# Block 0: transposes of the output weights and the gate product one slice further back in TensorE's queue

## Chip, cores and metric

The kernel runs on one core of a Trainium2 chip. The metric is the device time of one execution in microseconds (us). TensorE is named PE in the rows, its weight load PEld, VectorE DVE, ScalarE ACT, GpSimd POOL, and the queue that issues transfers SP.

## What is computed

A linear-attention recurrence (4 batches, 8 heads of 48, 768 steps), a gated feed-forward layer on the 3072 resulting rows, and a routed layer with 8 experts that picks one expert for each row:

```
for t in range(S):
    cur = np.einsum('bhd,bhe->bhde', u[None] * kt, vt)
    y[:, :, t] = np.einsum('bhd,bhde->bhe', rt, state + cur)
    state = w[None, :, :, None] * state + np.einsum('bhd,bhe->bhde', kt, vt)
...
g = x @ w_gate
silu = g * (1.0 / (1.0 + np.exp(-g)))
val = x @ w_val
return (silu * val @ w_out).astype(np.float32)
...
logits = x @ w_gate
e_idx = np.argmax(logits, axis=1)
...
    h = np.maximum(x[mask] @ w1[e], 0.0)
    ye = h @ w2[e]
    out[mask] = gate_w[mask, None] * eom[mask, e, None] * ye
```

## The kernel before

The 3072 rows are 24 tiles of 128; three tiles are a block, and there are 8 blocks. The feed-forward layer goes through 12 slices f of 128 hidden columns. Each slice of a block has gate products on TensorE into bank 3 (L494, nine matmuls), value products into bank 4 (L494, nine more), a silu on ScalarE (L502), its product with the value on VectorE (L503), a cast to the high part h on ScalarE (L505), a subtraction for the low part (L506, on GpSimd in block 0), and two slices later the down products into banks 0 to 2 (L513).

Block 0 also prepares the weights, once. They come as 64-bit words. Slice f is converted on VectorE by nine instructions (L214, L215, L216: `conv_a`) into a buffer `cv` of which there are two, one for even and one for odd slices. ScalarE casts the result to the high part of W (L232, the weight cast), GpSimd subtracts for the low part (L233: `conv_b`). So that the router's logits come out of the down products too, the output weights are multiplied with the router matrix G: three transposes on TensorE into bank 7 (L241) and a copy of them to `gt` on ScalarE (L243: `gate_a`); then three matmuls with G, also into bank 7 (L249, the gate product of the weights), small copies on ScalarE (L252, L253) and a small subtraction on GpSimd (L254: `gate_b`).

Between these steps lies the attention of the next block's three tiles (i = 3, 4, 5 in block 0): scaling of k and r on VectorE (L316), a diagonal (L334, then L343 on GpSimd or eight L341 on ScalarE), scores on TensorE into banks 6 and 7 in turn (L363), a masking of the diagonal's tile with them on VectorE (L368), output matmuls into bank 6 (L376, L390), a state product into bank 7 (L427), the evacuation of the output (L410 on ScalarE, L411 on VectorE), and the state update out of bank 7 (L441, L443).

Each engine carries out its instructions in the order in which the program writes them. That order is set by hand: a block has 24 slots, two to a slice. Slot 2f is written after the gate products of slice f, ahead of the down products of f-2 and the value products of f; slot 2f+1 after the silu, product and casts of slice f. `a_place` appends the attention's steps to the slots, and the lines below `if blk == 0` put the weights' steps in, mostly at the front of a slot. Semaphores make an instruction wait for its data and for the bank or buffer that it overwrites.

Of the kernel before, what the change touches and what calls it, by code (L numbers as in the profile page):

```python
# [28 lines left out]
NF = DFF // P  # L29
# [22 lines left out]
def kernel(  # L52
# [167 lines left out]
    def conv_a(f):  # L220
        for u in conv_steps(f):
            u()
# [3 lines left out]
    def conv_b(f, parts=(ALL,)):  # L226
        x = cvs[f]
        if f not in W:
            W[f] = wpool.tile([P, 2, FG], F32R, tag=f"W{f}", name=f"W{f}")
        for o in parts:  # L230
            hi, lo = W[f][:, 0, o], W[f][:, 1, o]
            act.copy(out=hi, in_=x[:, o])  # L232
            pool.tensor_tensor(out=lo, in0=x[:, o], in1=hi.bitcast(F32), op=ALU.subtract)  # L233
# [11 lines left out]
    def gate_b(f):  # L245
        t = gts.pop(f)
        wg = bank[7][:, DM : DM + 16]
        for c in range(KC):
            pe.matmul(wg, t[:, c * P : (c + 1) * P], G[:, c, :], start=(c == 0), stop=(c == KC - 1))  # L249
        hi, lo = W[f][:, 0, FW:], W[f][:, 1, FW:]  # L250
        x = apool.tile([P, 16], F32, tag="wg", name="wg", bufs=2)
        act.copy(out=x, in_=wg)  # L252
        act.copy(out=hi, in_=x)  # L253
        pool.tensor_tensor(out=lo, in0=x, in1=hi.bitcast(F32), op=ALU.subtract)  # L254
# [177 lines left out]
    def a_state_up(i, b):  # L432
        c = i // NB
        if c == TPB - 1:
            return
        m4 = bank[b][:, 0 : 4 * HD].rearrange("s (p e) -> s p e", p=4)
        for j in range(2):
            q = slice(64 * j, 64 * j + HD)
            sv, m = Sst[i % NB][q, :, j, 0:HD], m4[q]
            if c == 0:  # L440
                dve.tensor_copy(out=sv, in_=m)  # L441
            else:
                dve.tensor_tensor(out=sv, in0=m, in1=sv, op=ALU.add)  # L443
# [169 lines left out]
    def a_place(slots, i, first):  # L613
        e = 1 if i % BT == BT - 1 else 0
        if i + 1 < NT:
            slots[first].append(lambda: a_load(i + 1))
        if i < 2 * BT:
            slots[first + (i == BT)].append(lambda: a_scale(i))
            slots[first + 1].append(lambda: a_diag(i, BT < i))
            slots[first + 3 - e] += [lambda: a_keys(i), lambda: a_scores(i), lambda: a_mask(i)]  # L620
            slots[first + 5 - e] += [lambda: a_out(i), lambda: a_load_kr(i + 1), lambda: a_bonus(i + 1)]
            slots[first + 6].append(lambda: a_state_up(i, 7))
            return
        e = 0
        if i == 2 * BT:
            slots[first] += [lambda: a_scale(i), lambda: a_diag(i, False)]
            slots[first + 2] += [lambda: a_scores(i), lambda: a_next(i), lambda: a_load_kr(i + 1)]
        slots[first + 3 - e].append(lambda: a_keys(i))
        if i + 1 < NT:
            slots[first + 3 - e].append(lambda: a_bonus(i + 1))  # L630
            slots[first + 4 - e].append(lambda: a_scale(i + 1))
        slots[first + 5 - e].append(lambda: a_burst(i))
        if i + 1 < NT:
            slots[first + 5 - e].append(lambda: a_diag(i + 1, False))
            slots[first + 6 - e].append(lambda: a_next(i + 1))
        if i + 2 < NT:
            slots[first + 6 - e].append(lambda: a_load_kr(i + 2))
# [165 lines left out]
    with tc.manual_schedule():  # L803
# [56 lines left out]
        zts = []  # L860
        for blk in range(NBLK):
# [6 lines left out]
                for t in range(BT):  # L868
                    a_place(slots, (blk + 1) * BT + t, 8 * t)
            if blk == 0:  # L870
                slots[0][0:0] = [lambda: gate_b(0), lambda: conv_b(1, (GV, OUT)), lambda: gate_a(1), lambda: conv_a(2), lambda: a_state(0, 0)]
                slots[1][0:0] = [lambda: gate_b(1), lambda: conv_b(2), lambda: a_state(1, 1)]
                slots[2][0:0] = [lambda: gate_a(2), lambda: a_state(2, 2), lambda: gate_b(2)]
                for f in range(3, NF):
                    slots[2 * f - 5] += [lambda f=f: conv_a(f), lambda f=f: next_w(f + 2) if f > 3 else None]
                    slots[2 * f - 3].insert(0, lambda f=f: conv_b(f)); slots[2 * f - 3 + (f == 3)].insert(0, lambda f=f: gate_a(f))
                    slots[2 * f - 2].insert(0, lambda f=f: gate_b(f)) if f > 3 else slots[4].append(lambda: gate_b(3))
                slots[19].append(lambda: zts.append(late_consts()))
            else:
                for o, u in zip((4, 7, 7) if blk == NBLK - 1 else (12, 15, 15), c_units(blk - 1)):  # L880
                    slots[o].append(u)
                if blk == 1:
                    for i in range(16):
                        clear(2 * i, 2 + (2 * i) // 3)
                if 2 <= blk < 6:
                    for n in range(3):
                        for k, u in enumerate(scan_units(3 * (blk - 2) + n)):
                            slots[7 * n + 1 + 4 * k].append(u)
# [279 lines left out]
```

## Time and profile before

| what | before |
|---|---|
| median of 3 runs | 862.46 us (859.89 to 864.29) |
| the profiled execution, its own time | 861.56 us |
| its span, first to last instruction | 859.8 us |
| TensorE, matmuls busy | 821.9 us, 96% of the span |
| VectorE busy | 459.8 us, 53% |
| ScalarE busy | 271.2 us, 32% |
| GpSimd busy | 267.9 us, 31% |
| mean granted clock of TensorE | 0.985 |

Busy shares are means over the whole span, in which block 0 takes the time from about 34 to 135 us. The granted clock is a share of full speed: 1.00 is 2.4 GHz and 0.50 is 1.2 GHz.

### The profile page before, as it was taken

Reading aid. Unit: us, or ns where it says so; the run is one execution under the profiler, and the core shown is the slowest. Engines: PE = TensorE matmul, PEld = TensorE weight load, DVE = VectorE, ACT = ScalarE, POOL = GpSimd, SP = SyncE. Lnnn points to the kernel's source line nnn. Section 1 sums busy time; section 2 is a strip of 40 time slices with the busy share of each in tenths; the row PEclk is TensorE's granted clock in tenths of the full one; section 3 lists DMA queues with packets and bytes.
Section 4 is the critical chain, followed back from the end, with each engine's and each line's share of the span. In section 5 each row is a group of like instructions: output and inputs, shape, how many; then the busy total and the mean of one; then the engine's idle time right before and its main releaser. Section 6 shows DMA issues by size and latency. Waiting matters only on the chain.

```text
span 859.8 us, 13873 instructions
## 1 busy us (share of the span) xinstructions
PE 821.9 (96%) x5427; PEld 792.9 (92%) x5427; DVE 459.8 (53%) x945; ACT 271.2 (32%) x590; POOL 267.9 (31%) x241
## 2 busy tenths in 40 slices
PE   2888889999999999999999999999999999999996
PEld 2677789999999999999999999999999999999996
DVE  7898753354465456456455434243565565465541
ACT  2434342221222212212212221223454454444432
POOL 6756546223425335245244112010110210121022
PEclk9879989999999999999999999999999999999999
DMA  8615413853322323333323210410394444444201
GB/s 249 247 59 209 146 67 100 249 141 123 105 94 78 129 78 107 109 102 130 116 102 130 60 47 29 161 51 1 118 368 142 167 142 127 158 133 163 85 26 36
DMA packets 29769, 104.90 MB, mean 122 GB/s; under 512 B 5175, under 2 KB 14193, under 8 KB 26624
## 3 DMA queue, kind: packets, MB, share of 16 engines
q1 hardware_dynamic: 26368, 94.37, 34.0%
q0 software_dynamic: 3328, 9.56, 2.9%
q8 instruction: 45, 0.74, 0.4%
q14 instruction: 28, 0.23, 0.1%
HBM read 85.84 MB, written 16.41 MB: 119 GB/s over the span
## 4 chain that ended last, share of the span: by engine, by line
PE 84%; DVE 8%; DMA 2%; issue 2%; ACT 1%; SPq 1%; POOL 0%; POOLq 0%; DVEq 0%; ACTq 0%
PE bank L494 31%; PE bank L513 17%; PE bank L708 12%; PE bank L725 12%; PE bank L363 3%; PE bank L390 2%; PE bank L376 2%; DVE bank L215 2%; DVE bank L214 2%; DMA spare<-in_rkv_dram 2%; DVE cv L216 2%; PE bank L673 1%; PE bank L739 1%; SPq L415 1%; DVE krT L316 1%
## 5 line engine op out<-in xcount | busy, mean ns | idle before, releaser
L494 PE MATMUL bank<-xT,W 128*128 128x384 f32 x1728 | 331.4, 342 | 1.5 <-DMA xT<-stage 1.3
L494 PEld LDWEIGHTS bank<-xT,W 128*128 128x128 f32 x1728 | 305.1, 189 | 5.8 <-DMA xT<-stage 2.2
L513 PE MATMUL bank<-W,h 128*128 128x400 f32 x864 | 176.0, 348 | 0.0
L513 PEld LDWEIGHTS bank<-W,h 128*128 128x128 f32 x864 | 155.9, 189 | 0.5 <-issue 0.2
L505 ACT CAST h<-s 128x384 fp32r<-128x384 f32 x96 | 49.2, 513 | 328.4 <-DVE s L503 328.4
L503 DVE TENSOR_TENSOR s<-s,bank 128x384 f32<-128x384 f32 x96 | 53.2, 554 | 161.4 <-PE bank L494 148.6
L725 PE MATMUL bank<-hd,wf 128*128 128x416 f32 (+1 forms) x576 | 113.9, 344 | 0.0
L725 PEld LDWEIGHTS bank<-hd,wf 128*128 128x128 f32 x576 | 104.3, 188 | 0.7 <-DVE hd L712 0.2
L747 POOL DMA_INDIRECT out_dram<-yo,ix x32 | 35.0, 1095 | 200.6 <-DVE yo L743 174.0
L343 POOL TENSOR_TENSOR at<-ident,a 128x1024 f32<-128x1024 f32 x19 | 36.1, 1897 | 149.2 <-PE bank L494 118.2
L712 DVE SCALAR_TENSOR_TENSOR hd<-bank,hd 128x416 fp32r<-128x416 f32 (+1 forms) x64 | 36.7, 573 | 77.1 <-ACT hd L711 77.1
L506 DVE TENSOR_TENSOR h<-s,h 128x384 fp32r<-128x384 f32 x84 | 51.8, 616 | 48.7 <-ACT h L505 48.7
L657 DVE TENSOR_TENSOR wf<-raw,wf 128x768 fp32r<-128x768 f32 x64 | 61.1, 955 | 7.0 <-ACT wf L656 1.2
L502 ACT ACTIVATE s<-bank 128x384 f32<-128x384 f32 x96 | 47.2, 492 | 47.4 <-PE bank L494 47.4
L575 POOL DMA_INDIRECT xs<-rows,slot x24 | 23.8, 991 | 112.8 <-DVE slot L573 51.5
L711 ACT ACTIVATE hd<-bank 128x416 fp32r<-128x416 f32 (+1 forms) x64 | 32.3, 505 | 82.3 <-PE bank L708 81.9
L708 PE MATMUL bank<-xd1h,wf 128*128 128x416 f32 x192 | 58.2, 361 | 0.0
L656 ACT CAST wf<-raw 128x768 fp32r<-128x768 f32 x64 | 52.8, 825 | 0.0
L368 DVE COPY_PREDICATED at<-mask,bank 128x512 f32<-128x512 int32 x42 | 28.5, 732 | 38.7 <-POOL at L343 35.3
L708 PE MATMUL bank<-xd0h,wf 128*128 128x416 f32 x144 | 43.8, 362 | 0.0
L708 PEld LDWEIGHTS bank<-xd1h,wf 128*128 128x128 f32 x192 | 36.0, 188 | 0.5
L324 POOL TENSOR_TENSOR rkv<-rkv,ub 128x384 f32<-128x384 f32 x21 | 21.8, 1037 | 46.3 <-DMA rkv<-in_rkv_dram 46.3
(175 smaller groups left out, 946.9 us busy)
## 6 DMA issues: line engine op xcount, KB each, us to landing
raw<-in_w_dram SPq DMA_DIRECT2D x36, 768.0 KB, 4.4
raw<-in_w_dram SPq DMA_DIRECT2D x22, 1152.0 KB, 7.1
rkv<-in_rkv_dram SPq DMA_DIRECT2D x21, 576.0 KB, 5.4
krT<-in_krT_dram SPq DMA_DIRECT2D x42, 192.0 KB, 3.4
xs<-zt SPq DMA_DIRECT2D x32, 197.0 KB, 6.0
xr<-xs SPq DMA_DIRECT2D x6, 591.0 KB, 5.7
spare<-in_w_dram SPq DMA_DIRECT2D x2, 1152.0 KB, 9.4
xT<-stage SPq DMA_DIRECT2D x42, 48.0 KB, 2.1
```

Of the source, the lines that this page charges most:

```text
L343: pool.tensor_tensor(out=af, in0=bc(ident, 1, [P, NH, P]), in1=bc(a, 2, [P, NH, P]), op=ALU.mult)
L494: pe.matmul(ps[i], W[f][:, wl, o : o + P], x[:, xl, c, :], start=(c == 0 and n == 0), stop=(c == KC - 1 and n == 2),)
L502: act.activation(out=s, in_=g, func=AF.Silu)
L503: dve.tensor_tensor(out=s, in0=s, in1=v, op=ALU.mult)
L505: act.copy(out=h[:, 0], in_=s)
L506: (pool if blk == 0 else dve).tensor_tensor(out=h[:, 1], in0=s, in1=h[:, 0].bitcast(F32), op=ALU.subtract)
L513: pe.matmul(bank[t][:, 0 : DM + 16], h[:, hl, t * P : (t + 1) * P], W[f][:, wl, 2 * KC * P :], start=(f == 0 and n == 0), stop=(f == NF - ...
L656: act.copy(out=wf[:, 0], in_=raw[:, f])
L657: dve.tensor_tensor(out=wf[:, 1], in0=raw[:, f], in1=wf[:, 0].bitcast(F32), op=ALU.subtract)
L708: pe.matmul(ps, wf[:, wl, c * P : (c + 1) * P], xd[xl][:, c, 0:n], start=(i == 0), stop=(i == 3 * KC - 1))
L712: dve.scalar_tensor_tensor(h[:, 1, 0:n], ps, 0.0, h[:, 0, 0:n].bitcast(F32), ALU.max, ALU.subtract)
L725: pe.matmul(bank[c][:, 0:n], wf[:, wl, o : o + P], h[:, hl, 0:n], start=(f == 0 and i == 0), stop=(f == NEF - 1 and i == 2),)
```

## The change

The steps `gate_a` (transposes and copy gt) of slices 1 to 11 and `gate_b` (gate product of the weights) of the same slices go to later slots. For slices 4 to 11 `gate_a` goes from slot 2f-3 to slot 2f-1 and `gate_b` from 2f-2 to 2f; slices 1 to 3 move by one or two slots. `conv_a` and `conv_b` keep their slots. Within an odd slot `conv_b` of slice f+1 now comes first and `gate_a` of slice f second. Two things go with it: the state update of tile 5 moves from slot 22 to slot 20, and the constants of `late_consts` from slot 19 to slot 22.

```diff
-            slots[first + 6].append(lambda: a_state_up(i, 7))
+            slots[first + 6 - 2 * e].append(lambda: a_state_up(i, 7))
...
-                slots[0][0:0] = [lambda: gate_b(0), lambda: conv_b(1, (GV, OUT)), lambda: gate_a(1), lambda: conv_a(2), lambda: a_state(0, 0)]
-                slots[1][0:0] = [lambda: gate_b(1), lambda: conv_b(2), lambda: a_state(1, 1)]
-                slots[2][0:0] = [lambda: gate_a(2), lambda: a_state(2, 2), lambda: gate_b(2)]
-                for f in range(3, NF):
-                    slots[2 * f - 5] += [lambda f=f: conv_a(f), lambda f=f: next_w(f + 2) if f > 3 else None]
-                    slots[2 * f - 3].insert(0, lambda f=f: conv_b(f)); slots[2 * f - 3 + (f == 3)].insert(0, lambda f=f: gate_a(f))
-                    slots[2 * f - 2].insert(0, lambda f=f: gate_b(f)) if f > 3 else slots[4].append(lambda: gate_b(3))
-                slots[19].append(lambda: zts.append(late_consts()))
+                slots[0][0:0] = [lambda: gate_b(0), lambda: conv_b(1, (GV, OUT)), lambda: conv_a(2), lambda: a_state(0, 0)]
+                slots[1][0:0] = [lambda: gate_a(1), lambda: conv_b(2), lambda: a_state(1, 1)]
+                slots[2][0:0] = [lambda: gate_b(1), lambda: a_state(2, 2)]
+                for f in range(2, NF):
+                    if f > 2:
+                        slots[2 * f - 5] += [lambda f=f: conv_a(f), lambda f=f: next_w(f + 2) if f > 3 else None]
+                        slots[2 * f - 3].insert(0, lambda f=f: conv_b(f))
+                    slots[2 * f - 1].insert(0, lambda f=f: gate_a(f))
+                    slots[2 * f].insert(0, lambda f=f: gate_b(f))
+                slots[22].append(lambda: zts.append(late_consts()))
```

What this does to the queues is shown in three places. The first is TensorE around slot 3, from the gate products of slice 1 to the first scores of tile 3, before:

```order
L494 MATMUL bank3_64<-xT_259,W1_371 128x384 x9
L241 MATMUL bank7_68<-ident_69,cv_381 128x128 x3
L427 MATMUL bank2_63<-spare6_99,spare9_102 48x48 x8
L249 MATMUL bank7_68<-G_76,gt_456 128x16 x3
L494 MATMUL bank4_65<-xT_259,W1_371 128x384 x9
L363 MATMUL bank6_67<-krT_110 128x128
L363 MATMUL bank7_68<-krT_110 128x128
```

and in the changed kernel:

```order
L494 MATMUL bank3_64<-xT_259,W1_371 128x384 x9
L249 MATMUL bank7_68<-G_76,gt_407 128x16 x3
L427 MATMUL bank2_63<-spare6_99,spare9_102 48x48 x8
L494 MATMUL bank4_65<-xT_259,W1_371 128x384 x9
L241 MATMUL bank7_68<-ident_69,cv_376 128x128 x3
L363 MATMUL bank6_67<-krT_110 128x128
L363 MATMUL bank7_68<-krT_110 128x128
```

The transposes of slice 2 (cv_381 before, cv_376 after; the number is a buffer's) have gone behind the value products of slice 1 and stand directly ahead of the scores; the gate product that was in slot 2 is now that of slice 1.

The second place is ScalarE from the cast h of slice 2 (h_558 before, h_546 after), the end of slice 2, to the small copy of the gate product in slot 6, before:

```order
L505 CAST h_558<-s_555 128x384
L243 COPY gt_564<-bank7_68 128x384
L232 CAST W4_566<-cv_504 128x1152
L410 CAST xT_585<-bank6_67 128x3x128
L410 CAST stage_586<-bank6_67 128x128
L252 COPY wg_619<-bank7_68 128x16
```

and in the changed kernel:

```order
L505 CAST h_546<-s_543 128x384
L232 CAST W4_549<-cv_497 128x1152
L243 COPY gt_555<-bank7_68 128x384
L410 CAST xT_573<-bank6_67 128x3x128
L410 CAST stage_574<-bank6_67 128x128
L252 COPY wg_607<-bank7_68 128x16
```

The weight cast of slice 4 has come ahead of the copy gt, which is now that of slice 3 and not of slice 4. The same two have changed places in every odd slot from 3 on (in slot 3 the weight cast of slice 3 and the copy of slice 2).

The third place is TensorE from slot 19 on, behind the value products of slice 9, before:

```order
L241 MATMUL bank7_68<-ident_69,cv_1025 128x128 x3
L494 MATMUL bank3_64<-xT_259,W10_1011 128x384 x9
L249 MATMUL bank7_68<-G_76,gt_1089 128x16 x3
L376 MATMUL bank6_67<-krT_110,S1_107 128x128 x4
...
L494 MATMUL bank4_65<-xT_259,W10_1011 128x384 x9
L494 MATMUL bank3_64<-xT_259,W11_1091 128x384 x9
```

and in the changed kernel:

```order
L241 MATMUL bank7_68<-ident_69,cv_941 128x128 x3
L494 MATMUL bank3_64<-xT_259,W10_994 128x384 x9
L249 MATMUL bank7_68<-G_76,gt_1080 128x16 x3
L376 MATMUL bank6_67<-krT_110,S1_107 128x128 x4
...
L494 MATMUL bank4_65<-xT_259,W10_994 128x384 x9
L241 MATMUL bank7_68<-ident_69,cv_1013 128x128 x3
L494 MATMUL bank3_64<-xT_259,W11_1074 128x384 x9
L249 MATMUL bank7_68<-G_76,gt_1162 128x16 x3
```

Before, only the transposes and gate product of slice 11 stood here; now those of slice 10 stand in their place and those of slice 11 around the gate products of slice 11.

## Rows read from the trace of the kernel before

**Rows 1.** Stretches: length, busy us of each engine (instructions), clock, DMA share, GB/s.

```profile
33.70:63.00 29.30, 25.17 (x163) 22.11 (x163) 27.79 (x53) 9.33 (x23) 18.76 (x16) 0.77 0.37 142
...
131.30:600.00 468.70, 467.39 (x3235) 456.38 (x3234) 220.99 (x456) 109.19 (x231) 150.12 (x123) 1.00 0.33 103
```

**Rows 2.** Waits of VectorE, 33 to 120 us: waited for, us in total, times, longest.

```profile
DVE xT L411 <- ACT xT L410: 5.1, 2, 2.7
DVE at L368 <- PE bank L363: 2.4, 2, 2.0
...
DVE s L503 <- PE bank L494: 0.2, 1, 0.2
```

**Rows 3.** Waits of TensorE, 33 to 125 us.

```profile
PE bank L241 <- DVE S L441: 2.4, 1, 2.4
PE bank L241 <- DVE cv L216: 2.3, 3, 1.0
```

**Rows 4.** Timeline, slots 0 to 4: start, length, engine, line, operation, idle before.

```profile
46.24 0.56 DVE L503 TENSOR_TENSOR s<-s,bank 128x384 f32<-128x384 f32 x1
...
53.59 1.93 PE L363 MATMUL bank<-krT 64*128 64x128 f32 x16
...
55.92 0.55 DVE L503 TENSOR_TENSOR s<-s,bank 128x384 f32<-128x384 f32 x1
...
56.39 1.35 DVE L368 COPY_PREDICATED at<-mask,bank 128x512 f32<-128x512 int32 x2
...
63.17 0.56 DVE L503 TENSOR_TENSOR s<-s,bank 128x384 f32<-128x384 f32 x1 [0.24 <-PE bank L494]
```

**Rows 5.** Timeline, slots 9 to 13.

```profile
84.07 1.73 PE L494 MATMUL bank<-xT,W 128*128 128x384 f32 x9
...
86.36 0.55 DVE L503 TENSOR_TENSOR s<-s,bank 128x384 f32<-128x384 f32 x1
...
87.36 0.47 ACT L243 COPY gt<-bank 128x384 f32<-128x384 f32 x1
...
87.89 1.16 PE L363 MATMUL bank<-krT 64*128 64x128 f32 x14 [0.36 <-ACT gt L243]
...
88.87 1.36 DVE L368 COPY_PREDICATED at<-mask,bank 128x512 f32<-128x512 int32 x2 [1.96 <-PE bank L363]
...
92.95 1.75 PE L494 MATMUL bank<-xT,W 128*128 128x384 f32 x9
```

**Rows 6.** Timeline, slots 9 and 10.

```profile
81.52 1.16 ACT L232 CAST W<-cv 128x1152 fp32r<-128x1152 f32 x1
...
81.67 0.84 PE L249 MATMUL bank<-G,gt 128*128 128x16 f32 x6 [0.34 <-ACT gt L243]
...
82.57 2.45 ACT L341 ACTIVATE at<-ident,a 128x128 f32<-128x128 f32 x8
```

**Rows 7.** Timeline, slots 18 to 20.

```profile
117.57 2.07 PE L363 MATMUL bank<-krT 64*128 64x128 f32 x14 [2.20 <-ACT wg L252]
...
124.66 0.49 PE L241 MATMUL bank<-ident,cv 128*128 128x128 f32 x3
...
124.93 0.56 DVE L503 TENSOR_TENSOR s<-s,bank 128x384 f32<-128x384 f32 x1 [4.26 <-PE bank L494]
...
126.57 0.74 PE L249 MATMUL bank<-G,gt 128*128 128x16 f32 x6
```

**Rows 8.** Stretches of half a us: columns as in the first group.

```profile
41.50:42.00 0.50, 0.50 (x5) 0.50 (x5) 0.50 (x1) 0.05 (x1) 0.50 (x2) 0.58 0.35 111
...
116.50:117.00 0.50, 0.00 (x0) 0.00 (x0) 0.47 (x2) 0.50 (x3) 0.50 (x1) 0.67 0.00 0
123.00:123.50 0.50, 0.50 (x3) 0.50 (x3) 0.00 (x0) 0.00 (x0) 0.00 (x0) 0.50 0.00 0
```

**Rows 9.** Timeline: scaling of k and r on VectorE.

```profile
47.46 2.05 DVE L316 TENSOR_TENSOR krT<-krT,WT 128x1024 f32<-128x1024 f32 x1
...
79.01 1.22 DVE L316 TENSOR_TENSOR krT<-krT,WT 128x1024 f32<-128x1024 f32 x1
```

## The prediction

> **What bounds the kernel now.** I read four views in turn. The table of stretches [rows 1] says where the engines are full: from 131.3 to 600 us TensorE is busy 467.39 of 468.70 us, so there every microsecond of lateness is simply carried to the end. Between 33.7 and 63.0 us it is VectorE that is full (27.79 of 29.30 us; its instructions stand end to end), while TensorE works at a mean clock of 0.77. The change touches only block 0 (about 34 to 135 us), so the question is what it does to VectorE's chain up to the switch at about 117.6 us, and to TensorE's after it.
>
> The waits of VectorE [rows 2] show that between 33 and 120 us it stands still for little: 5.1 us in front of the evacuation of attention output (L411), 2.4 us in front of the masking of scores (L368), 0.2 us in front of a silu product (L503, the last step of a slice; "product f" below). Nowhere else does TensorE hold VectorE up. The waits of TensorE [rows 3] show what the change can remove: the transposes (L241) stood 2.3 us in all for VectorE's conversion (L216).
>
> **The change part by part.** *What it removes.* The 2.3 us of L241 are waits of an engine that is not the bound while VectorE is full: each ends with VectorE's own step, and TensorE catches up before VectorE needs it again. I cost the gain at nothing; its upper bound is the 2.3 us.
>
> *What it adds.* As the order on ScalarE shows, the copy gt of slice f used to stand right behind the cast h; now the weight cast W of slice f+1 (L232) stands between them. And that copy is awaited by more than the gate product: scores go into bank 7 as well, so their second matmul waits until ScalarE has read the transposes out of it.
>
> *Slots 0 to 2.* The copy gt of slice 1 now stands behind the cast h of slice 0, which waits for VectorE's product at 46.24 [rows 4]; so gate product 1 starts at about 46.24 + 1.53 = 47.8 (the 1.53 is worked out below), and TensorE stands for it. Value products 1 follow within 2.5 us of that and have until product 1 at 55.92 to end: VectorE's three conversions and two state updates in between hide all of it. Without that cover it would be the 4 to 5 us of TensorE's wait.
>
> *Slot 3.* Before, scores (L363) had long been done when VectorE got to the mask: product at 55.92, mask at 56.39, 0.47 later [rows 4]. The new order puts transposes 2 directly ahead of these scores. What that does is seen in slot 11, where the old order had it already [rows 5]: product 86.36, copy gt 87.36, scores 87.89, mask 88.87. So product to scores is 1.53, product to mask 2.51 us, with the copy directly behind the cast h. In the new order the weight cast comes in between; from its start to that of the next ScalarE instruction are 82.57 - 81.52 = 1.05 us [rows 6]. So in slot 3 the mask starts 2.51 + 1.05 = 3.56 us after the product instead of 0.47: 3.09 later. VectorE waited 0.24 us for TensorE in front of product 2, at 63.17 [rows 4], and that takes up as much; 3.09 - 0.24 = 2.85 us are left, at full clock. VectorE has no idle time before that to give, and everything behind the mask on its queue (three parts of conversion 4, the product of slice 2) moves with it.
>
> The clock is the unknown here. It fell to its lower level (1.2 GHz, 0.50 in the rows) at about 41.6, was there when the old scores ran (sixteen in 1.93 us, [rows 4]), and fell again between 116.5 and 117, to stay there beyond 123 us [rows 8]. In the new order TensorE stands from about 54.5 (the 53.59 of the old scores, plus transposes) to 55.92 + 1.53 + 1.05 = 58.50 us. At 117 the fall came in a wait of 2.2 us [rows 7]; here it would be 4. At half clock fourteen scores take 2.07 instead of 1.16 us [rows 7, 5], a factor of 1.78. From the scores to the end of the value products TensorE has 92.95 + 1.75 - 87.89 = 6.8 us of work at full clock [rows 5]. In the stretch at 117 the clock came back some 5.9 us after work resumed at 117.57; if so here, 5.9/1.78 = 3.3 us of it is done by 64.4, the other 3.5 ends at 67.9, and the product of slice 2 starts at about 68.0 instead of 63.17: 4.8. If the clock is back after half of that time, 61.5 + 5.1 = 66.6: 3.5. Bounds 2.85 and 4.8; I take 4.5, near the row that shows a return.
>
> *Slots 4 to 8.* The gate products come 0.6 us later than now in most slices (1.05 for the cast, less the 0.4 in which TensorE had to finish the gate matmuls anyway). VectorE's conversions (nine instructions each) with krT scaling or state updates behind them cover it. No charge; uncovered it would be 0.6 a slice.
>
> *Slots 9 to 11.* Gate product 5 goes from 81.67 to 82.72 [rows 6], so the value products that started at 84.07 and took 1.73 start 1.05 later and end at 86.85; VectorE was free for them at 86.36 [rows 5], so it waits: 0.6 (0.1 for the hand-over). In slot 11 the copy is once more behind a weight cast: 1.05. Together 1.65; without the cover of conversion 7 it would be 2.1. Slots 13 and 15 have the same ScalarE work in another order: nothing.
>
> *From 117.6 on.* Now TensorE is full. Transposes 10 and 11 and their gate products stand after the scores of slot 18, where before there was only slice 11: 0.49 + 0.74 us by [rows 7], less the overlap of pipelined ends; I take 0.9. And the gate product of slot 20 waits for a copy behind a weight cast: 124.93 + 1.53 + 1.05 = 127.51 instead of 126.57, 0.94. Without the matmuls of the gate as cover it would be the full 1.05. Together 1.85. The constants moved from slot 19 to 22 lie on GpSimd, which waits for work there; the clears that use them come in block 1. GpSimd's small subtraction (L254) comes a slice later, long before the down product that reads it. The state update moved from slot 22 to 20 is ahead of value products that take 1.7 us and hide it. No DMA is passed.
>
> *Sum.* 4.5 + 1.65 + 1.85 = 8.0 us on the profiled execution, whose own time is 861.56 (0.9 below the median 862.46): 869.6. With the bounds of the clock alone 6.35 to 8.3.
>
> **The rivals.** *The clock is kinder.* If the second low stretch, 117.57 to 123.5, is gone because the waits before it are now in two pieces (gate product, then scores), it saves 5.9 x (1 - 1/1.78) = 2.6 us: 867.0; if slot 3 also runs at full clock, 865.3. For it: TensorE waited 2.4 us for a state update [rows 3] and no fall shows there. Against it: the wait for the eight ScalarE diagonals stays.
>
> *More goes wrong.* A further low stretch costs another 2.6. Or GpSimd's subtraction of the weights, which starts earlier now, meets the krT scaling on VectorE: that took 2.05 at 47.46, with GpSimd's L506 running, and 1.22 at 79.01 [rows 9], so 0.8 in each of two slots, on VectorE's chain. The Trainium skill (SBUF — State Buffer, "SBUF: two separate sides") says the port pair shared by the two is locked for a whole instruction; the trace agrees in that the scaling at 47.46 takes 0.83 us more. Against it: the subtraction now ends sooner, before the scaling starts. Times: 871 to 874.
>
> *The late mask is absorbed (not slower).* VectorE's idle time in front of L411 and L368, 7.5 us, swallows the 4.5 and the 1.65. That decides if the evacuations in slots 5 and 13 hang on TensorE alone and not on the preceding product. Only the tail is left: 863.4. Against it: the ScalarE cast that they wait for stands behind the cast h, gt and W of the same slot, all of which start with that product.
>
> *Faster.* TensorE no longer stands at L241 [rows 3], keeps its clock, and the 2.3 and the 2.6 come off without a charge: 856.7. Against it: VectorE is full in just these stretches, and it would need the mask not to wait for the copy.
>
> **How the numbers follow.** Forecast 0.50 (8.0; 868 to 871 by itself); kinder clock 0.22; worse 0.13; absorbed 0.08; faster 0.04; 0.03 for what I don't see. The predicted time is the forecast's, 869.6. The range runs from 865.5, which lets in nearly all of the kinder clock and leaves out absorbed and faster (0.12), to 873.5, which leaves out the far end of the worse ones. One measurement tells 0.5%, 4.3 us, from no change: slower means above 866.8. That is the forecast, the worse cases and over half of the kinder clock: 0.78. The same: the rest of it and the absorbed case, 0.18. Faster 0.04.
>
> **What would show it.** Right: the mask of slot 3 starts about 3.6 us (4.4 at half clock) behind the product, with VectorE waiting there; the gate product of slot 9 waits some 1.4 us for gt; the mask of slot 11 starts 3.6 us behind its product; the products of slot 20 wait about 1 us. The first stretch without TensorE idle begins some 8 us later than 117.6. Wrong: scores of slot 3 that start before the copy gt; VectorE idle in front of L411 that shrinks; a clock of 1.00 from 58 us on would make it too high by 1.7, and one of 1.00 at 117 to 123 by 2.6.

## The result, and the profile after

The changed kernel took 870.03 us (median of 6 runs, 869.08 to 872.18) where the kernel before, on the same chip, took 864.01 (6 runs): ratio 1.0083, 95% interval 1.0058 to 1.0107. In a second group of runs (the ninth experiment) it was 870.81 to 862.24, ratio 1.0103 (1.0079 to 1.0127). It is slower in both groups, by 6.0 and by 8.6 us between the medians (0.8 and 1.0%). The forecast was 869.6.

Block 0 began 0.70 us earlier in the profiled execution of the changed kernel (first evacuation L411 at 33.05, before at 33.75), so the two windows below start 0.7 us earlier and some 7.2 us later than those of [rows 1].

Stretches of the changed kernel, columns as in [rows 1]:

```profile
33.00:62.30 29.30, 18.71 (x129) 16.99 (x130) 24.27 (x47) 7.70 (x17) 17.95 (x14) 0.78 0.37 141
138.50:607.20 468.70, 466.75 (x3232) 455.19 (x3231) 219.89 (x453) 109.39 (x234) 148.82 (x124) 1.00 0.33 103
```

VectorE, full in the first stretch before (27.79 of 29.30 us), has lost 3.5 us of it. From 138.5 on TensorE is full again, so what block 0 lost is carried on. The waits of VectorE and of TensorE (33 to 132 us) answer to [rows 2, 3]:

```profile
DVE at L368 <- PE bank L363: 7.4, 2, 3.8
DVE xT L411 <- ACT xT L410: 4.8, 2, 2.4
DVE s L503 <- PE bank L494: 1.8, 3, 1.0
```

```profile
PE bank L363 <- ACT gt L243: 6.3, 2, 4.4
...
PE bank L241 <- DVE cv L216: 0.6, 1, 0.6
```

The transposes' wait for the conversion fell from 2.3 to 0.6, as the change could do; in its place scores wait 6.3 us for the copy gt, and the masks behind them 7.4 instead of 2.4. The timeline shows both places; first slot 3 ([rows 4]):

```profile
55.20 0.55 DVE L503 TENSOR_TENSOR s<-s,bank 128x384 f32<-128x384 f32 x1
...
56.21 1.15 ACT L232 CAST W<-cv 128x1152 fp32r<-128x1152 f32 x1
...
57.26 0.47 ACT L243 COPY gt<-bank 128x384 f32<-128x384 f32 x1
...
57.78 2.07 PE L363 MATMUL bank<-krT 64*128 64x128 f32 x14 [4.37 <-ACT gt L243]
59.55 1.35 DVE L368 COPY_PREDICATED at<-mask,bank 128x512 f32<-128x512 int32 x2 [3.79 <-PE bank L363]
...
59.78 3.25 PE L494 MATMUL bank<-xT,W 128*128 128x384 f32 x9
...
67.06 0.55 DVE L503 TENSOR_TENSOR s<-s,bank 128x384 f32<-128x384 f32 x1 [0.95 <-PE bank L494]
```

Product, weight cast, copy gt, scores, mask: the chain as forecast, the mask 4.35 us behind the product where it was 0.47. The scores took 2.07 us and the nine gate products 3.25: TensorE was at half clock. Slots 9 to 11 ([rows 5]):

```profile
86.64 0.84 PE L249 MATMUL bank<-G,gt 128*128 128x16 f32 x6 [0.85 <-ACT gt L243]
...
90.88 0.56 DVE L503 TENSOR_TENSOR s<-s,bank 128x384 f32<-128x384 f32 x1 [0.51 <-PE bank L494]
...
93.47 1.92 PE L363 MATMUL bank<-krT 64*128 64x128 f32 x14 [1.95 <-ACT gt L243]
95.01 1.35 DVE L368 COPY_PREDICATED at<-mask,bank 128x512 f32<-128x512 int32 x2 [3.58 <-PE bank L363]
...
101.95 0.56 DVE L503 TENSOR_TENSOR s<-s,bank 128x384 f32<-128x384 f32 x1 [0.32 <-PE bank L494]
```

Half a microsecond waited in front of product 5, and again the mask behind scores behind gt; here too the scores ran slowly (1.92, 1.16 before). From slot 18 to the down products of slice 9, answering to [rows 7]:

```profile
123.90 1.66 PE L363 MATMUL bank<-krT 64*128 64x128 f32 x14 [1.14 <-ACT wg L252]
...
130.11 0.56 DVE L503 TENSOR_TENSOR s<-s,bank 128x384 f32<-128x384 f32 x1 [3.51 <-PE bank L494]
...
132.69 0.84 PE L249 MATMUL bank<-G,gt 128*128 128x16 f32 x6 [0.79 <-ACT gt L243]
...
141.64 1.87 PE L513 MATMUL bank<-W,h 128*128 128x400 f32 x9
```

and the same down products in the kernel before:

```profile
134.50 1.78 PE L513 MATMUL bank<-W,h 128*128 128x400 f32 x9
```

They are 7.14 us later, 7.84 counted from the block's first evacuation. Clock rows of half a microsecond show it low after the wait in slot 3, and falling in slot 11:

```profile
57.50:58.00 0.50, 0.22 (x2) 0.22 (x4) 0.00 (x0) 0.23 (x1) 0.50 (x1) 0.50 0.00 0
...
93.50:94.00 0.50, 0.50 (x6) 0.50 (x8) 0.00 (x0) 0.00 (x0) 0.50 (x1) 0.67 0.91 387
```

The clock was low from 45.9 to 52.7, 56.1 to 63.0, 93.7 to 97.1 and 124.4 to 127.8 us; before, from 41.6 to 55.2 and from 116.7 to 123.5.

### The profile page after: what moved, and what is told of

Read it like the earlier page. It is cut to its first block, busy times and chain, and to the rows that moved or that the text cites. A ratio compares the mean times of both kernels' runs of the same rounds, so it can differ in the third digit from the quotient of the medians.

```text
span 870.4 us, 13867 instructions
## 1 busy us (share of the span) xinstructions
PE 822.7 (95%) x5427; PEld 793.7 (91%) x5427; DVE 461.9 (53%) x945; ACT 270.9 (31%) x590; POOL 267.8 (31%) x241
## 4 chain that ended last, share of the span: by engine, by line
PE 79%; DVE 9%; issue 5%; ACT 3%; DMA 1%; SPq 1%; POOL 0%; POOLq 0%; DVEq 0%
PE bank L494 31%; PE bank L513 17%; PE bank L708 11%; PE bank L725 11%; PE bank L363 3%; PE bank L390 2%; PE bank L376 2%; DVE bank L215 2%; DVE bank L214 2%; DVE cv L216 1%; SPq L415 1%; DVE krT L316 1%; PE bank L673 1%; PE bank L739 1%; DVE s L503 1%
## 5 line engine op out<-in xcount | busy, mean ns | idle before, releaser
L503 DVE TENSOR_TENSOR s<-s,bank 128x384 f32<-128x384 f32 x96 | 53.2, 555 | 164.9 <-PE bank L494 155.4
```

Of the source, the lines that this page charges most:

```text
L503: dve.tensor_tensor(out=s, in0=s, in1=v, op=ALU.mult)
```

## Experiments

For each kernel the table has the time, its ratio to runs of before in the same group with the 95% interval, and four lengths in us out of one profile, as differences of starts (product f is the silu product L503 of slice f): product 1 to product 2 (slots 3 and 4), product 4 to product 6 (slots 9 to 12), product 8 to the down products of slice 9 (slots 17 to 22), and the block's first L411 to these down products.

| kernel | us | ratio | 1 to 2 | 4 to 6 | 8 to down 9 | block |
|---|---|---|---|---|---|---|
| before | 862 to 864 | 1 | 7.25 | 15.28 | 21.91 | 100.75 |
| changed | 870.03 | 1.0083 (1.0058-1.0107) | 11.86 | 17.89 | 22.72 | 108.59 |
| 1 gt first | 868.76 | 1.0083 (1.0062-1.0105) | 10.53 | 17.82 | 21.69 | 106.13 |
| 2 early slices only | 870.17 | 1.0088 (1.0068-1.0108) | 15.63 | 15.28 | 21.92 | 109.09 |
| 3 late slices only | 867.16 | 1.0077 (1.0047-1.0108) | 7.24 | 17.92 | 22.72 | 104.44 |
| 4 filled wait | 868.57 | 1.0076 (1.0056-1.0096) | 10.12 | 16.94 | 22.76 | 107.56 |
| 5 gt first, filled | 865.03 | 1.0038 (1.0025-1.0051) | 9.06 | 15.31 | 21.69 | 103.02 |
| 6 scores first | 867.79 | 1.0061 (1.0037-1.0085) | 7.00 | 14.44 | 22.73 | 104.65 |
| 7 before, scores freed | 858.66 | 0.9961 (0.9945-0.9976) | 7.26 | 13.36 | 20.09 | 98.00 |
| 8 change, scores freed | 863.96 | 1.0018 (1.0002-1.0034) | 7.00 | 13.38 | 19.86 | 98.45 |
| 9 changed again | 870.81 | 1.0103 (1.0079-1.0127) | 11.64 | 17.86 | 22.73 | 108.34 |
| 10 before, filled wait | 859.80 | 0.9967 (0.9952-0.9981) | 8.79 | 15.29 | 19.21 | 99.58 |
| 11 small steps | 862.07 | 0.9999 (0.9980-1.0017) | 7.23 | 15.27 | 21.87 | 100.65 |
| 12 before, freed further | 857.89 | 0.9939 (0.9925-0.9953) | 8.78 | 13.35 | 17.04 | 96.46 |

The theory was that of the prediction: the copy gt, late on ScalarE, holds up scores that share bank 7, and so masks, on VectorE's chain; and the clock falls in these waits. The first rival was that the clock alone costs, the second that the late mask is absorbed.

**1. The copy ahead of the weight cast.**

```diff
-                        slots[2 * f - 3].insert(0, lambda f=f: conv_b(f))
+                        slots[2 * f - 3].insert(1, lambda f=f: conv_b(f))
```

> The changed kernel, but in the odd slots from 3 on the copy gt stands on ScalarE ahead of the weight cast W again; the slots are those of the change. Theory (the copy's place in ScalarE's queue delays the scores that share bank 7, and the gate products): 1.05 us come back in slot 3, 0.6 in slot 9, 1.05 in slot 11 and 0.9 in slot 20, together 3.6 us below the changed kernel (870.0), so 866.4; the mask of slot 3 starts 1.05 us nearer to its product than the 4.35 of the changed kernel. Rival (the low clock in the wait is the whole cost; TensorE still waits for the copy and still falls): within 1 us of 870.0.

By the time alone this can't be told from the changed kernel. The lengths can: slot 3 gave back 1.33 and slots 17 to 22 1.03, but slots 9 to 12 nothing. The mask of slot 3 came 1.05 us nearer to its product (3.30 us behind it, 4.35 in the change), as expected. The mask of slot 11 came nearer too (2.50, 4.13 in the change), and then this happened:

```profile
90.08 1.16 PE L363 MATMUL bank<-krT 64*128 64x128 f32 x14 [1.36 <-ACT gt L243]
91.06 1.36 DVE L368 COPY_PREDICATED at<-mask,bank 128x512 f32<-128x512 int32 x2 [1.96 <-PE bank L363]
...
91.16 2.91 PE L494 MATMUL bank<-xT,W 128*128 128x384 f32 x9
...
100.13 0.56 DVE L503 TENSOR_TENSOR s<-s,bank 128x384 f32<-128x384 f32 x1 [2.43 <-PE bank L494]
```

```profile
91.50:92.00 0.50, 0.50 (x4) 0.50 (x3) 0.50 (x2) 0.00 (x0) 0.50 (x1) 0.58 0.82 350
```

The clock fell after a wait of 1.36 us and stayed low until 98.4, and product 6 waited 2.43 us for TensorE. Order and clock are two costs, and here the second took what the first gave. The fifth run separates them.

**2. Slices 1 to 3 alone** (`gate_a` of 1, 2 in slots 1, 3 and `gate_b` in 2, 4; slice 3 in slot 4; the rest as before).

```diff
...
-                slots[2][0:0] = [lambda: gate_a(2), lambda: a_state(2, 2), lambda: gate_b(2)]
...
+                slots[2][0:0] = [lambda: gate_b(1), lambda: a_state(2, 2)]
+                slots[3].insert(0, lambda: gate_a(2))
...
+                slots[4][0:0] = [lambda: gate_b(2), lambda: gate_a(3)]
+                slots[4].append(lambda: gate_b(3))
```

> Slices 1 to 3 in the slots of the change, slices 4 to 11 in those of before. Theory (slot 3 alone carries over half of the cost): product 2 comes 4.6 us later against product 0, and nothing after slot 4 gives it back: 868.6 against 864.0 of before. Rival (the idle time of VectorE in front of the masks and evacuations, 7.5 us, takes the late mask up): 864 to 865.

Not absorbed: the second rival falls. But the size missed, 870.17 for 868.6 (7.9 us above before in its group, 862.27, where 4.6 were expected), and the kernel isolates less than I thought. Slot 4 now has two gate products and a transposition, and the clock fell once more, from 68.4 to 71.8:

```profile
65.99 0.55 PE L241 MATMUL bank<-ident,cv 128*128 128x128 f32 x3 [0.31 <-ACT wg L252]
67.11 0.84 PE L249 MATMUL bank<-G,gt 128*128 128x16 f32 x6 [0.57 <-ACT gt L243]
67.80 2.84 PE L513 MATMUL bank<-W,h 128*128 128x400 f32 x9
```

Product 1 to 2 is 8.4 us longer than before, not 4.6. Everything behind it is as before (15.28, 21.92): nothing is given back.

**3. Slices 4 to 11 alone** (with the two steps that go with them).

```diff
...
-                    slots[2 * f - 3].insert(0, lambda f=f: conv_b(f)); slots[2 * f - 3 + (f == 3)].insert(0, lambda f=f: gate_a(f))
-                    slots[2 * f - 2].insert(0, lambda f=f: gate_b(f)) if f > 3 else slots[4].append(lambda: gate_b(3))
...
+                    if f > 3:
+                        slots[2 * f - 1].insert(0, lambda f=f: gate_a(f))
+                        slots[2 * f].insert(0, lambda f=f: gate_b(f))
...
```

> Slices 1 to 3 in the slots of before, slices 4 to 11 (and the two steps that go with them) in those of the change. Theory: slots 9 to 11 cost 0.6 + 1.6 (the mask of slot 11 at half clock) and slot 20 costs 1.9, less what the shorter low stretch behind slot 18 gives back (1 us): 3 us above before, 867. Rival (the later slices cost nothing, since their copies are hidden; all is slot 3): 864.0. Second rival (the two parts are not additive: without the late slot 3 the state update of tile 5 and the transposes meet other work): outside 865 to 869.

867.16 is the number of the theory, but by luck: it was reckoned from 864.0, and before took 862.27 in this group. So the time is 4.9 us above before, not 3, with a wide spread (863.81 to 874.08); the block is 3.69 above. The lengths of slots 9 to 12 and 17 to 22 are those of the changed kernel to 0.03 us. With the 4.61 of slot 3 the parts make 8.3; together they measured 7.84. Most of the difference lies with a low-clock stretch from 71.4 to 74.8 us that the changed kernel does not have: products 2 to 4 took 17.41 us for 16.98.

**4. TensorE kept at work in the wait of slot 3.**

```diff
+                slots[3].insert(2, lambda: [pe.matmul(bank[6][:, 0:BN], W[1][:, 0, 0:P], xT[0][:, 0, 0, :], start=True, stop=True) for _ in range(22)])
```

> The changed kernel plus 22 matmuls of 128x384 whose result nobody reads, in slot 3 behind the transposes of slice 2 and ahead of the scores, into bank 6, which the scores then overwrite: TensorE works through its wait for gt. Theory (part of the cost of slot 3 is the low clock in that wait): granted clock 1.00 from 53 to 66 us, fourteen scores in 1.16 instead of 2.07 us, product 2 without a wait for TensorE; 1.75 us below the changed kernel: 868.3. Rival (VectorE's own chain behind the mask sets product 2, at either clock): only the 0.9 of the shorter scores come back at most, 869.1 or more. Second rival (the clock falls in spite of the work): 870.0, with the fill taking over 6 us and the scores later.

```profile
55.03 4.24 PE L880 MATMUL bank<-xT,W 128*128 128x384 f32 x22
...
59.99 1.16 PE L363 MATMUL bank<-krT 64*128 64x128 f32 x14 [0.31 <-ACT gt L243]
```

```profile
55.50:66.00 10.50, 10.19 (x68) 9.63 (x67) 7.09 (x15) 2.71 (x6) 4.88 (x5) 1.00 0.00 0
```

The clock stayed full, the scores took 1.16, product 2 waited for nobody, and from product 1 to 2 it was 10.12 us: 2.87 above before, where the prediction worked out 2.85 for full clock. So of the 4.61 us of slot 3 the order costs 2.87 and the low clock 1.74, and the rival that the clock alone costs falls. Slots 9 to 12, where nothing was filled, show the same split. The scores of slot 11 waited the same 1.95 us for gt as in the changed kernel, but this time the clock stayed full:

```profile
91.34 0.55 DVE L503 TENSOR_TENSOR s<-s,bank 128x384 f32<-128x384 f32 x1 [0.50 <-PE bank L494]
...
93.92 1.16 PE L363 MATMUL bank<-krT 64*128 64x128 f32 x14 [1.95 <-ACT gt L243]
94.91 1.36 DVE L368 COPY_PREDICATED at<-mask,bank 128x512 f32<-128x512 int32 x2 [3.01 <-PE bank L363]
```

```profile
91.00:98.00 7.00, 5.05 (x40) 4.54 (x39) 3.49 (x6) 2.40 (x6) 4.60 (x4) 1.00 0.49 171
```

The mask came 3.57 us behind its product, and products 4 to 6 took 16.94, 1.66 above before. The time by itself shows less: 868.57 is near the 868.3 expected, but its interval overlaps that of the changed kernel. The profiled execution also lost 1.65 us ahead of product 0 (last section).

**5. Both: gt first, and the waits of slots 3 and 11 filled.**

```diff
-                        slots[2 * f - 3].insert(0, lambda f=f: conv_b(f))
+                        slots[2 * f - 3].insert(1, lambda f=f: conv_b(f))
...
+                slots[3].insert(1, lambda: [pe.matmul(bank[6][:, 0:BN], W[1][:, 0, 0:P], xT[0][:, 0, 0, :], start=True, stop=True) for _ in range(14)])
+                slots[11].insert(1, lambda: [pe.matmul(bank[6][:, 0:BN], W[5][:, 0, 0:P], xT[0][:, 0, 0, :], start=True, stop=True) for _ in range(7)])
```

> The kernel of the first experiment (copy gt ahead of the weight cast W) plus matmuls of 128x384 that nobody reads, behind the transposes in slot 3 (14 of them) and slot 11 (7 of them), so that TensorE works through its wait for gt. In the first experiment the order gave back 1.05 us at the mask of slot 11, but a low-clock stretch of 6.8 us after it cost 2.5 at product 6. Theory (order and clock are two separate costs): from product 1 to product 2 9.0 to 9.5 us (7.25 before, 11.86 in the change, 10.53 in the first experiment), from product 5 to product 6 9.1 (9.07 before, 11.07 changed, 11.57 first experiment), and block 0 some 2 us above before. Rival (the clock falls whatever stands in the wait): product 6 again 11 us or more behind product 5.

9.06 and 9.07 us (product 5 to 6), as expected; slots 9 to 12 are back at the 15.31 of before. A fall of the clock at 76 us, where nothing was filled, cost 0.9 in front of product 4. The block is 2.27 above before, the time 0.38%. The interval lies wholly below that of the changed kernel: the order on ScalarE and the clock in its waits are most of the loss.

**6. The scores ahead of the transposes.**

```diff
+                ga, gb = {2: 4, 6: 12}, {2: 5, 6: 13}
...
+                    head = [lambda f=f: gate_b(f) for f in range(2, NF) if gb.get(f, 2 * f) == n]
+                    a = [lambda f=f: gate_a(f) for f in range(2, NF) if ga.get(f, 2 * f - 1) == n]
```

> The changed kernel with the scores of slots 3 and 11 ahead of the transposes: gate_a of slices 2 and 6, and conv_a of slices 4 and 8 behind it, go to the front of slots 4 and 12, gate_b of slices 2 and 6 to the front of slots 5 and 13. Theory (the scores wait for gt through bank 7): the mask of slot 3 starts 0.5 us behind product 1 and product 2 comes 7.3 to 8 us behind it (11.86 in the change); the mask of slot 11 0.5 us behind product 5, product 6 about 7.5 to 9 us behind it (11.07). Block 0 then costs the tail of slots 9 and 18 to 20 alone, within 1.5 us of before or below it: 861 to 864 against 862.3. Rival (the work that the change added to TensorE's queue costs by itself, wherever the scores stand): 3 us or more above before.

```profile
55.73 1.33 DVE L368 COPY_PREDICATED at<-mask,bank 128x512 f32<-128x512 int32 x2
...
62.26 0.55 DVE L503 TENSOR_TENSOR s<-s,bank 128x384 f32<-128x384 f32 x1
...
63.48 0.90 PE L241 MATMUL bank<-ident,cv 128*128 128x128 f32 x3 [2.01 <-ACT wg L252]
...
66.82 0.56 DVE L411 TENSOR_TENSOR xT<-bank,xT 128x384 fp32r<-128x384 f32 x1 [4.01 <-ACT xT L410]
```

The places named came out as the theory said: the mask 0.47 us behind product 1, product 2 after 7.00 us, product 6 7.62 behind product 5. The cost of slot 3 is gone without leaving out any work. The total missed (867.8 for 861 to 864), and by the time alone the rival's sign, 3 us or more above before, is there. The places say otherwise: with the gate product now in slots 5 and 13, the next transposes wait 2.0 us for its small copy, which ScalarE reaches behind the cast h, and output and evacuation stand behind them (4.01 us instead of 2.39; 5.17 in slot 13). That cost 1.6 us between products 2 and 4 and 2.6 between 6 and 8, with a low clock in both (63.0 to 66.4, 97.2 to 100.6). It is the same wait on a reader of bank 7, at a new place. The eighth run asks again whether the added work costs by itself.

**7. The kernel before, with its own two such waits taken away.**

```diff
-                    slots[2 * f - 3].insert(0, lambda f=f: conv_b(f)); slots[2 * f - 3 + (f == 3)].insert(0, lambda f=f: gate_a(f))
+                    slots[2 * f - 3].insert(0, lambda f=f: conv_b(f)); slots[2 * f - 3 + (f in (3, 7))].insert(0, lambda f=f: gate_a(f))
...
+                for f in (7, 10):
+                    slots[2 * f - 1].insert(0, lambda f=f: gate_b(f))
```

> The kernel before, with two steps put behind the scores: gate_a of slice 7 goes from slot 11 to the front of slot 12 and its gate_b to slot 13, and gate_b of slice 10 goes from slot 18 to the front of slot 19. Theory: the mask of slot 11, 2.51 us behind its product before, comes 0.5 behind it, and the scores of slot 18 no longer stand 2.2 us behind the small copy after the eight diagonals, so the low-clock stretch there (117 to 123.5) goes too: product 6 some 1.5 to 2 us earlier, product 9 another 2 to 3: 858 to 859.5 against 862.3. Rival (the waits were slack of VectorE, whose conversion fills the time up to the next product): 861.5 to 862.5.

858.66, faster than before by 0.39%, within the forecast. Product 6 comes 1.92 us nearer to product 4; 1.0 of that is lost again between products 6 and 8 (18.18 for 17.16), where transposes now wait 1.90 us for the small copy of slot 13. At slot 18 the scores now follow at once:

```profile
111.78 1.55 PE L363 MATMUL bank<-krT 64*128 64x128 f32 x16
...
118.24 0.84 PE L249 MATMUL bank<-G,gt 128*128 128x16 f32 x6 [1.50 <-DVE at L368]
```

but the gate product waits for the mask, the clock fell there (119.2 to 122.6), and slots 17 to 22 gave 1.8 us, less than the 2 to 3 expected.

**8. The change with the same freedom** (as the sixth, and gt ahead of the weight cast).

```diff
...
+                ga, gb = {2: 4, 6: 12, 10: 20}, {2: 5, 6: 13, 9: 20, 10: 21}
...
+                    slots[n][0:0] = head + a + c + late
...
```

> The changed kernel with the scores of slots 3, 11 and 18 free of the weights' steps, and gt ahead of the weight cast everywhere: gate_a of slice 2, 6, 10 in slots 4, 12, 20, gate_b of slices 2, 6, 9, 10 in slots 5, 13, 20, 21. Theory: nothing is left of the 4.6 of slot 3, the 2.2 of slots 9 to 11 and the 0.9 of slot 20, and the old wait of 2.0 us at the mask of slot 11 and of 2.2 at the scores of slot 18 are gone too: 858 to 860 against 862.3. Rival (the transposes now wait for the mask, since it reads bank 7, and TensorE loses there what VectorE gains): 861 to 864.

In this profile the block agrees with the theory: 98.45, 2.30 below before and 0.45 above the seventh, so here the work that the change added does not cost by itself. The time does not agree: 863.96, inside the rival's 861 to 864. The profiled execution is not a typical one, since it took 860.15 at a mean granted clock of 0.995. Three executions at 0.991 or more took 859.7 to 861.9 us, the nine at 0.983 to 0.987 took 862.5 to 866.0. So the miss goes with the clock; where it fell in those nine no trace shows, and for them the rival is not excluded. The profile itself lost 3.3 us after block 0 against that of before, 1.70 of them in one gap behind the branch ahead of the last stage (last section). Why the rest came I did not find.

**9. The changed kernel again,** with no edit.

> The changed kernel once more, for a second profile of the same instructions beside the same runs of before as the three others of this group. Theory: the block's own shift is the order's doing, so product 2 comes 11.5 to 12 us behind product 1 again and the down products of slice 9 some 7 to 8.5 us later than before, counted from the block's first evacuation; what differs between two profiles is the start of the block (33 to 35 us), which of the later waits the clock falls in, and the 2 us behind the branch after 640 us. Time 868.5 to 870. Rival (the low-clock stretches fall at random and made most of the 7.8 us): a shift outside 6.5 to 9.

The lengths agree with the first profile to 0.22 us, and 7.59 us for the block, with the low stretches at the same places to 0.5 us: in two profiles out of two the sign of the rival of a chance did not come. The time is 0.8 above the upper end given.

**10. The kernel before, its wait of slot 18 filled.**

```diff
+                slots[18].insert(1, lambda: [pe.matmul(bank[6][:, 0:BN], W[8][:, 0, 0:P], xT[0][:, 0, 0, :], start=True, stop=True) for _ in range(11)])
```

> The kernel before plus 11 matmuls of 128x384 that nobody reads, in slot 18 between the gate product of slice 10 and the scores, into bank 6: TensorE works through the 2.2 us in which it waits for the small copy behind the eight diagonals. Theory (the low stretch from 117 to 123.5 us costs 2.6 us of TensorE's work at a place where TensorE sets the end): clock 1.00 there, the product of slice 9 and all behind it 2 to 2.6 us earlier, 859.7 to 860.2 against 862.2. Rival (the mask on VectorE sets that product): 862.2, with VectorE no longer waiting for TensorE in front of it.

```profile
117.48 2.19 PE L878 MATMUL bank<-xT,W 128*128 128x384 f32 x11
...
120.24 1.16 PE L363 MATMUL bank<-krT 64*128 64x128 f32 x14 [0.16 <-ACT wg L252]
```

```profile
117.00:124.50 7.50, 7.34 (x51) 6.78 (x51) 5.50 (x10) 3.79 (x12) 4.26 (x4) 1.00 0.00 0
```

The clock stayed full, slots 17 to 22 are 2.70 us shorter and the time is 0.33% below before: eleven useless matmuls make the kernel faster. That is the price of the second low stretch, put at 2.6 in the prediction.

**11. The two small steps alone.**

```diff
-            slots[first + 6].append(lambda: a_state_up(i, 7))
+            slots[first + 6 - 2 * e].append(lambda: a_state_up(i, 7))
...
-                slots[19].append(lambda: zts.append(late_consts()))
+                slots[22].append(lambda: zts.append(late_consts()))
```

> The kernel before with only the two steps that go with the change: the state update of tile 5 in slot 20 and not 22, the constants in slot 22 and not 19. Theory (costed at nothing: 1.7 us of value products hide the update, GpSimd waits anyway): 862.2, within 0.2% of before. Rival (the update ahead of product 10 delays it, or the clears of block 1 start late): 0.5 us or more above before, with VectorE's product 10 later.

No change (0.9999; block 0.10 shorter).

**12. The seventh taken further,** with the constants in slot 22.

```diff
...
+                slots[19][0:2] = []
+                slots[20][0:1] = [lambda: gate_b(10), lambda: gate_a(NF - 1), lambda: conv_b(NF - 1)]
+                slots[20].append(lambda: gate_b(NF - 1))
...
```

> The faster variant of before (gate_a of slice 7 in slot 12, its gate_b in 13) with the steps of the last two slices moved as well: gate_b of slice 10, gate_a and conv_b of slice 11 at the front of slot 20, behind the gate products of slice 10, gate_b of slice 11 at the end of slot 20, the constants in slot 22. Theory: in that variant TensorE stood 1.5 us for the mask ahead of the gate product and fell to half clock (3.07 us for nine gate products instead of 1.8); now the gate products lie beside the mask, TensorE keeps its clock, and the copy wg is not behind a weight cast: the down products of slice 9 come 2 to 2.5 us earlier than in that variant (98.0 us behind the block's first evacuation), 856 to 857 against 862.2. Rival (the transposes behind the small copies wait as long as the gate product did before): 858.5 as that variant.

```profile
119.08 3.31 PE L494 MATMUL bank<-xT,W 128*128 128x384 f32 x18
122.34 0.84 PE L249 MATMUL bank<-G,gt 128*128 128x16 f32 x6
```

The gate products lie beside the mask, the gate product waits for nobody, slots 17 to 22 are 3.05 us shorter than in the seventh. A fall of the clock in slot 4 (61.9 to 65.3), which before and the seventh do not have with the same instructions there, took half of that back in this profile (8.78 for 7.26). The time, 857.89, is 1 us above what was expected. It beats before by 0.61% and, across groups, the changed kernel by about 1.4 to 1.6%; from the seventh (another group, intervals that overlap) its time is not told apart.

## Why the prediction was right, step by step

- *What it removes* was rightly costed at nothing: the wait of the transposes for the conversion fell by 1.7 us and no product came earlier for it.
- *Slots 0 to 2*: gate product 1 waited 4.85 us for gt, as much as foretold, and product 1 stayed where it was (22.17 and 22.15 us behind the block's start). The cover held.
- *Slot 3*: forecast 4.5, measured 4.61 and, in the second profile, 4.39. The fourth run splits it into 2.87 of order and 1.74 of clock, as the working had done (2.85 and the rest). The clock came back 5.2 us after work resumed, not the 5.9 that was borrowed from slot 18; that made little difference.
- *Slots 4 to 8*, costed at nothing: products 2 to 4 took 16.98 us before and 17.00 after.
- *Slots 9 to 11*: a mis-sized term. Forecast 1.65, measured 2.61. The 0.6 in front of product 5 is there (0.61); the mask was 1.62 later instead of 1.05, and product 6 another 0.38. The working took full clock there; the wait of 1.95 us for gt was followed by a low stretch that the kernel before did not have. In the fourth run the same wait was followed by none, and the slots cost 1.66: the order was sized right and the clock left out. The fifth run, with the wait filled and gt first, shows all of it gone. One sign missed: the gate product of slot 9 waited 0.85 us for gt, not 1.4, though it started 1.06 later against product 4, as the working had it (1.05).
- *From 117.6 on*: mis-sized the other way. Forecast 1.85, measured 0.81. The extra matmuls and the wait in slot 20 cost 1.96 (from product 9 to the down products), but the low stretch at slot 18 was 3.4 us long instead of 6.8 and gave back 1.15. That is not quite half of the rival of the kinder clock, whose price of 2.6 the tenth run confirms (2.70). Why the stretch is shorter is not shown; that the wait is now in two pieces can't be all, since in the fifth run scores waited 2.19 us in one piece there and the stretch was 3.4 us as well. Of the signs, the gate product of slot 20 waited 0.79 us (some 1 us was said), and the full stretch began at 123.90, 6.3 us later and not 8, and was broken once more by these 0.79.
- *The sum* of 8.0 against 7.84 and 7.59 in the block is thus right with two errors of about 1 us that cancel, both of the clock. That 869.6 comes so near to 870.03 has luck in it besides: the sum was put on an execution of 861.56 us, while the runs of before beside the result had a median of 864.01, so that the medians lie 6.0 us apart in the first group and 8.6 in the second.
- *The rivals*: the absorbed mask is out (second and fourth run; the waits in front of L411 were 4.8 us for 5.1). A meeting of GpSimd's subtraction with the krT scaling cost VectorE nothing: the scalings of tiles 4 and 5 took 1.22 us again, that of tile 3 2.04 as before. In slot 1, which the prediction did not count, a subtraction did come earlier and met the scaling of tile 3 (48.13; the scaling ran from 46.75 to 48.79), but it was the subtraction that got longer (3.16 for 2.64). The faster case needed a mask that does not wait for gt, and the mask did wait (first and sixth run).

What stays open is behind the block. Both profiles of the changed kernel lose 2.5 and 3.5 us more after it than the one of before, 1.9 of them at the branch. A loss of 1.5 us or more there is in six of the eight profiles of kernels with the later slices moved (all but the fourth and fifth run) and in none of the six others, so it seems to go with the change. But no experiment was made on it, and the medians, 6.0 and 8.6 us apart with 7.84 and 7.59 in the block, do not show as much. Whether it belongs to the change was not settled.

## What to carry to other kernels

When a step is moved in an in-order queue, follow its readers: here a copy of 0.47 us on ScalarE, moved behind a cast of 1.15, held up scores that had no data in common with it, only the place in bank 7, and those held up the engine that was full. Whether a wait of TensorE costs anything depends on who needs its work next: the 1.7 us that the change took away in front of L241 brought nothing. Where TensorE's work is needed, a wait costs its length and then, if the clock falls, 0.9 to 2.7 us more in these runs; filling a wait of 2.2 us with useless work gave back 2.70. Taking two such waits out of the old order made it 0.4% faster, and 0.6% with the last two slices moved too; the waits for the conversion were 2.3 us, 0.27%, in all.

## What was not expected of the hardware

**The clock falls after short waits, and not always at the same place.** In the first run 1.36 us of waiting was followed by 6.8 us at half clock. At the scores of slot 11 a wait of 1.95 us was followed by a low stretch in the changed kernel and by none in the fourth run. The kernel before and the tenth run have the same instructions up to slot 18, yet in the tenth the clock was low from 61.5 to 64.9 and product 2 came 1.54 us later. Executions of one kernel spread with it: in the third run the one of 874.08 us had a mean granted clock of 0.978, the one of 863.81 us 0.986, and the eighth run falls into two groups by it.

**A tiny VectorE instruction lost 1.7 us in a meeting with GpSimd.** The check of the decay (L178, 4 elements a row) meets GpSimd's weight subtraction (L233). First the changed kernel, then the fourth run:

```profile
39.19 0.16 DVE L178 TENSOR_TENSOR wT<-wT,pw 128x4 f32<-128x4 f32 x1
39.21 2.81 POOL L233 TENSOR_TENSOR W<-cv,W 128x768 fp32r<-128x768 f32 x2 [0.51 <-ACT W L232]
```

```profile
39.74 2.80 POOL L233 TENSOR_TENSOR W<-cv,W 128x768 fp32r<-128x768 f32 x2 [0.51 <-ACT W L232]
39.76 1.83 DVE L178 TENSOR_TENSOR wT<-wT,pw 128x4 f32<-128x4 f32 x1
```

In the fourth run VectorE's took 1.83 us instead of 0.16 and ended with the first of GpSimd's two pieces (41.59 and 41.57), and all products moved by 1.65. The Trainium skill (SBUF — State Buffer, "SBUF: two separate sides") says that the port pair of the two is locked for a whole instruction by whichever starts first; that common end agrees. Who was first can't be read from these starts: GpSimd's stands 15 ns ahead in the fourth run, but it stands 4 to 12 ns ahead in five other profiles too, before among them, and VectorE's took 0.16 there:

```profile
39.89 2.81 POOL L233 TENSOR_TENSOR W<-cv,W 128x768 fp32r<-128x768 f32 x2 [0.51 <-ACT W L232]
39.89 0.16 DVE L178 TENSOR_TENSOR wT<-wT,pw 128x4 f32<-128x4 f32 x1
```

**A gap of 1.7 to 2.0 us behind the branch ahead of the last stage**, in which TensorE waited for nothing that the profile shows, is in 5 of the 14 profiles: both of the changed kernel, and the first, sixth and eighth run, all built on it. The row is of the changed kernel:

```profile
641.66 0.45 PE L708 MATMUL bank<-xd1h,wf 128*128 128x416 f32 x1 [1.94 <-issue]
```

In the profile of before the same matmuls follow at once. Its cause is open.
